# A retention block and a dense block in one kernel: loading order and order of work of the first microseconds

## The chip, the cores and the metric

The kernel runs on one core of a Trainium2 chip. The metric is the device time of one execution in microseconds; three runs of the kernel before gave 627.72, 628.25 and 628.29, median 628.25. The profile comes from one execution of its own, which took 627.76.

The engines in the views: PE is TensorE's matmul and PEld its weight load, DVE is VectorE, ACT ScalarE, POOL GpSimd, SP SyncE, which issues most of the DMAs. "Batch" below is one of the four batch entries.

## The reference

Four batch entries of 768 tokens with 8 heads of 64 pass a recurrent retention, then a dense block of 512 to 2048 to 512 with a leaky ReLU between. All is float32, but the weights arrive as float64 and are turned into float32 on the chip.

```python
gamma = 1.0 - 2.0 ** (-5.0 - np.arange(H, dtype=np.float32))
for t in range(S):
    state = gamma[None, :, None, None] * state + np.einsum('bhd,bhe->bhde', k[:, :, t], v[:, :, t])
    y[:, :, t] = scale * np.einsum('bhd,bhde->bhe', q[:, :, t], state)
x = np.ascontiguousarray(attn_out.transpose(0, 2, 1, 3)).reshape(B * S, H * D)
h = x @ w_in
g = np.maximum(0.01 * h, h)
out = g @ w_out
```

## The kernel before

The tokens are cut into six chunks of 128 for each batch. A chunk's output is a sum of two parts: tokens of earlier chunks through the state, and tokens of its own chunk through scores, q times k masked by causality, times v. The decay is taken out of the products: v is scaled by a table that depends on head and token (`decay_v`, L160), and the result by another (`gq`, in `tokens_taken`, L303). Both tables are made on the chip from a small input, `decay`, of 8 rows of 948 numbers, one row for each head. Matmuls with selector rows spread them over the 128 partitions: three small ones into `tables` (L934 to L938), copied by ScalarE into `dec` (L941), and one of 512 columns into `spread` (L946), copied into the front of `dec` (L950). These matmuls contract over all 128 partitions, so the 120 partitions without a head are set to zero.

The first chunk, on which the change works, has no state yet. For each batch b: `score(0,b)` is 32 small matmuls, `masked(0,b)` one VectorE operation of 128x768 out of PSUM, `decay_v(0,b)` scales v in place on GpSimd, `values(0,b)` are 32 matmuls of the masked scores with v, and `taken(0,b)` moves the result through VectorE, times gq, into the dense block's input x. Scores and values share two PSUM rooms (tag "att") in turn, so that a score of a later batch reuses the room of an earlier value once that is taken.

The weights come in pieces of 512 KB of float64. ScalarE makes the exponents of a piece (`next_powers`, three activations: L595, L599, L600). VectorE makes the mantissas: `begin_mantissas` is L607 and L612, with a given operation in between; `end_mantissas` is L619, which needs ScalarE's exponents, and then issues the load of a later piece. `next_mantissas` is both.

Most of the kernel uses Strassen-like schemes for the dense block, but the first quarter of the hidden units of chunk 0 is computed plainly by `direct` (L701), in four steps; step n reads weight piece n, and each call of `next(steps)` puts one step of four matmuls of 256 columns (two batches of 128) into PE's order. `th` says which two batches.

The schedule is written out by hand (`manual_schedule`): each engine executes its own instructions in the order of the program, and waits come from the data. The order at the start of the program is thus what the change edits. The loads of L882 to L901 go out on SP's queue in the order of the program, the decay rows on ScalarE's. `keep_busy` (L914) puts matmuls on zeros into PE's order while nothing has arrived.

Of the kernel before, what the change touches and what calls it, by code (L numbers as in the profile page):

```python
# [15 lines left out]
AF = mybir.ActivationFunctionType  # L16
# [6 lines left out]
def kernel(  # L23
# [14 lines left out]
    nc = tc.nc  # L38
    NC = S // C
    DM = H * D  # L40
    HP = H // 2
    NU = DF // 512
    N = B * C // 2
# [15 lines left out]
    dec = const.tile([128, HP * C + NC * H + HP], FP32, name="dec")  # L59
# [27 lines left out]
    def block(k, i):  # L87

        if k < N_UNITS - 1:
            return unit(k)[:, PLACE.get(i, i) if k % 2 else i]  # L90
        return units[k][i // 2][:, i % 2] if i < 6 else last_s4[:, 0]
# [3 lines left out]
    step = dec[:, HP * C + NC * H :]  # L95
# [24 lines left out]
    def load_qk(c, b, queue=nc.sync):  # L120
        queue.dma_start(out=heads[c, b][0], in_=qk[c, b])

    def load_v(c, b, queue=nc.sync):
        queue.dma_start(out=heads[c, b][1][:, 1], in_=kv[c, b][:, 1])
# [35 lines left out]
    def decay_v(c, b, engine=nc.gpsimd, behind=None):  # L160
        v = vals[c, b] if c >= JOINED else heads[c, b][1][:, 1]
        if engine is not nc.scalar:
            op = engine.tensor_tensor(out=v, in0=v,  # L163
                                      in1=gk[c].unsqueeze(2).to_broadcast([128, H, D]),
                                      op=ALU.mult)
            if behind is not None:
                tc.add_manual_dep(op.ins, behind.ins.name, IN_ORDER, reason="one port for both")
        else:
            for h in range(H):
                engine.activation(v[:, h], v[:, h], AF.Identity, scale=gk[c][:, h : h + 1])  # L170
# [9 lines left out]
    def score(c, b):  # L180

        ps = two_banks(f"ap_{c}_{b}").rearrange("p j a t -> p j (a t)")[:, :, 0:NS]
        scores[c, b] = ps.rearrange("p j (m n t) -> p j m n t", n=3, t=C // 2)
        scores_to(heads[c, b][0], [scores[c, b][:, j] for j in range(2)])
# [29 lines left out]
    def masked(c, b):  # L214
        am = new_am(c, b)
        nc.vector.tensor_tensor(
            out=am.rearrange("p j m n t -> p j m (n t)"),
            in0=scores[c, b].rearrange("p j m n t -> p j m (n t)"),
            in1=mask.rearrange("p n t -> p (n t)").unsqueeze(1).unsqueeze(1)
                .to_broadcast([128, 2, HP // 2, 3 * C // 2]), op=ALU.mult)  # L220
        scores[c, b] = am
# [20 lines left out]
    def values(c, b):  # L242
        if (c, b) not in sums_at:
            sums_at[c, b] = apart(two_banks(f"yp_{c}_{b}"))
        last_values(c, b)
        first_values(c, b)
# [51 lines left out]
    def taken(c, b, xb):  # L298

        tokens_taken(c, b, xb)  # L300
        state_taken(c, b, for_state(sums_at[c, b]))
# [232 lines left out]
    def load_piece(n, place=None):  # L534
        if n >= N_PIECES:
            return
        if not f64:
            nc.sync.dma_start(out=piece(n), in_=weights[n].rearrange("p (h n) -> p h n", h=2))
            return
        if place is None:  # L540
            tag, bufs = ("raw", 3) if n < N_PIECES - 4 else (("qk", "kv")[n % 2], AHEAD)
            raws[n] = work.tile([128, W], I64, tag=tag, bufs=bufs, name=f"raw{n}")
        else:
            raws[n] = place.bitcast(I64)
        nc.sync.dma_start(out=raws[n], in_=weights[n])

    def next_powers(scratch=None, between=None):
        n = done["powers"]
        done["powers"] += 1
        if n < N_PIECES and f64:  # L550
            powers(n, scratch, between)
        elif between is not None:
            between()

    def begin_mantissas(between=None):

        mantissas_begun(done["mantissas"], between)

    def end_mantissas():
        n = done["mantissas"]  # L560
        done["mantissas"] += 1
        op = mantissas_ended(n)
        if n != 3:
            load_piece(n + 4 if n < 3 else n + 3)
        if n == N_PIECES - 1:
            new_pair(2)
            for b in range(2):
                heads[2, b] = [work.tile([128, 2, HP, C], FP32, tag="qk", bufs=AHEAD,
                                         name=f"qk_2_{b}")]
            load_qk(2, 0)  # L570
            load_qk(2, 1)
            of_pair(2, 0, 1)
            of_pair(2, 0, 0)
        if n % 4 == 3 and n > 7:
            add_sums(n // 4)
        return op
# [121 lines left out]
    def temp(name, at):  # L698
        return work.tile([128, 2, N], FP32, tag=name, name=f"{name}_{at}")

    def direct(c, u, x, g, th):  # L701

        banks = [ffs.tile([128, 2, N], FP32, tag="ff", bufs=4, name=f"d{r}_{c}_{th}")
                 for r in range(2)]
        for step in range(4):
            kh, k = divmod(step, 2)
            for r in range(2):
                for i in range(2):
                    nc.tensor.matmul(  # L709
                        banks[r][:, i, :], lhsT=block(2 * u, r + 2 * kh)[:, k, ts(i, 128)],  # L710
                        rhs=x[:, 2 * kh + th, k, :], start=(step == 0 and i == 0),
                        stop=(step == 3), skip_group_check=True)
                if step == 3:
                    nc.scalar.activation(g[:, 2 * r + th], banks[r], AF.Prelu, alpha=0.01)
            yield

    filled = mask.rearrange("p n t -> p (n t)").bitcast(BF16)[:, 0:C]

# [159 lines left out]
    x, t = xs[0]  # L878
    rows = t[:, 1:3].rearrange("p i k n -> p (i k n)")[:, 0 : decay.shape[1]]
    nothing = t[:, 0, 0, 0:64].bitcast(BF16)  # L880
    half = decay.shape[1] // 2
    load_qk(0, 0)  # L882
    load_qk(0, 1)
    nc.vector.memset(t[:, 0, 0, 0:64], 0.0)
    nc.gpsimd.memset(rows[:, :half], 0.0)
    nc.vector.memset(rows[:, half:], 0.0)
    nc.scalar.dma_start(out=rows[0:H], in_=decay)
    load_v(0, 0)
    load_v(0, 1)
    load_piece(0)  # L890
    load_piece(1)
    load_qk(0, 2)
    load_v(0, 2)
# [10 lines left out]
    for s in range(2):  # L904
        part = mask[ts(s, 64), 0 : 3 - s : 2 - s]
# [4 lines left out]
    parts = [new_g(0, 0)]  # L910
# [3 lines left out]
    def keep_busy(n):  # L914
        for _ in range(n):
            nc.tensor.matmul(idle.rearrange("p i (two n) -> p (i two) n", two=2), lhsT=nothing,
                             rhs=nothing.unsqueeze(1).to_broadcast([128, 4, 128]),
                             start=True, stop=True, skip_group_check=True)
# [3 lines left out]
    n_gq = HP * C  # L922
# [5 lines left out]
    def scratch(name, n):  # L928
        return work.tile([128, 2, N], FP32, tag=name, name=f"{name}_x{n}")

    keep_busy(10)
    score(0, 0)
    n_gk, n_old = NC * H, JOINED * H
    nc.tensor.matmul(tables[:, 0, 0:n_old], lhsT=by_head, rhs=powers_of[:, 0:n_old], start=True,  # L934
                     stop=True, skip_group_check=True)
    nc.tensor.matmul(tables[:, 0, n_old:n_gk], lhsT=in_order, rhs=powers_of[:, n_old:],
                     start=False, stop=True, skip_group_check=True)
    nc.tensor.matmul(tables[:, 0, n_gk : n_gk + HP], lhsT=place, rhs=g_step, start=False,  # L938
                     stop=True, skip_group_check=True)
    masked(0, 0)  # L940
    nc.scalar.copy(out=dec[:, n_gq:], in_=tables[:, 0, 0 : n_gk + HP])  # L941
    decay_v(0, 0)
    score(0, 1)
    decay_v(0, 1)
    masked(0, 1)
    nc.tensor.matmul(spread.rearrange("p i n -> p (i n)"), lhsT=place, rhs=g_q, start=True,  # L946
                     stop=True, skip_group_check=True)
    values(0, 0)
    values(0, 1)
    nc.scalar.copy(out=dec[:, 0:n_gq], in_=spread.rearrange("p i n -> p (i n)"))  # L950
    next_powers(scratch("m5", 0))
    begin_mantissas(lambda: taken(0, 0, x))
    taken(0, 1, x)
    end_mantissas()
    next_powers(scratch("u2", 1))
    score(0, 2)
    steps = direct(0, 0, x, parts[0][1], 0)
    next(steps)
    converted = next_mantissas()
    decay_v(0, 2, behind=converted)  # L960
# [760 lines left out]
def _decay(H, D, NC):  # L1721

    import numpy as np

    lg = np.log1p(-(2.0 ** (-5.0 - np.arange(H))))
    t = np.arange(1, C + 1)
    gq = np.exp(lg[:, None] * t[None, :]) / math.sqrt(D)
    gq = gq.reshape(H // 4, 2, 2, C).transpose(1, 2, 0, 3).reshape(2, -1)
    step = np.exp(C * lg).reshape(H // 4, 2, 2).transpose(1, 2, 0).reshape(2, -1)
    place = np.concatenate([np.repeat(np.eye(2), 64, axis=1), gq, step], axis=1)  # L1730
    place = np.concatenate([place, np.zeros((H - 2, place.shape[1]))])
    in_order = np.exp(-lg[:, None] * t[None, :])
    by_head = in_order.copy()
    by_head[swapped(H)] = np.roll(by_head[swapped(H)], C // 2, axis=1)
    powers = [np.diag(np.exp(-c * C * lg)) for c in range(NC)]
    return np.concatenate([by_head, in_order, *powers, place], axis=1).astype(np.float32)

def _layout(q, k, v, w_in, w_out):

# [63 lines left out]
```

## Time and profile before

| | us |
|---|---|
| median of three runs | 628.25 |
| the profiled execution | 627.76 |
| its span, first to last instruction | 625.9 |
| matrix engine (PE) busy in the span | 620.0 |
| VectorE busy | 520.0 |
| ScalarE busy | 285.5 |
| GpSimd busy | 147.4 |

A span has 1.86 us less than the profiled execution's own time; the rest is before the first and after the last instruction. In a timeline a line gives the start from the beginning of the span, the length, the engine, the line of the program, the operation, what is written and read, and in brackets the time in which the engine stood idle before it and what ended that. In the list of waits a line gives the engine and the line that waited, what it waited for, the microseconds in total, the number of times and the longest. In the chain of waits a line gives start, length and what was under way in that stretch.

The transfers of the first microseconds, from the trace's DMA view (issue, and microseconds from issue to landing; for the two v blocks the trace was asked in pairs, so the smaller and the larger value stand):

| transfer | KB | issued | to landing |
|---|---|---|---|
| qk of batch 0 | 512 | 0.80 | 3.6 |
| qk of batch 1 | 512 | 1.25 | 4.8 |
| decay rows (ScalarE's queue) | 29.6 | 1.59 | 4.69 |
| v of batch 0 | 256 | 1.72 | 5.2 |
| v of batch 1 | 256 | 2.19 | 6.1 |
| weight piece 0 | 512 | 2.66 | 6.9 |
| weight piece 1 | 512 | 3.18 | 7.7 |
| qk of batch 2 | 512 | 3.67 | 8.5 |
| v of batch 2 | 256 | 4.41 | 8.4 |

### The profile page before, as it was taken

How to read it: one execution, taken by the hardware profiler on the slowest of the kernel's cores; microseconds unless marked ns; L12 is line 12 of the kernel's file. 1: busy time of each engine (PE TensorE's matmuls, PEld its weight loads, DVE VectorE, ACT ScalarE, POOL GpSimd, SP SyncE). 2: the span in 40 equal slices, each digit the busy share in tenths (PEclk: the TensorE clock that was granted, in tenths of full speed). 3: DMA queues.
4: the chain of work that ended last, by engine and by line, in shares of the span. 5: the costliest groups of instructions: out<-in, count | busy, mean ns of one | idle time of the engine just before them, and what ended most of it. 6: DMA issues, size and time to landing. Idle time of an engine off the chain costs nothing.

```text
span 625.9 us, 15366 instructions
## 1 busy us (share of the span) xinstructions
PE 620.0 (99%) x6410; PEld 571.8 (91%) x6410; DVE 520.0 (83%) x799; ACT 285.5 (46%) x546; POOL 147.4 (24%) x152
## 2 busy tenths in 40 slices
PE   8999999999999999999999999999999999999998
PEld 5888888888888889998999999999999999999997
DVE  5689769889979976779888868789968789989897
ACT  4876556347444114352433433634614435545641
POOL 2000000000010110105133052331250711379473
PEclk9999999999999999999999999999999999999999
DMA  8941426547772996496976996988478568688601
GB/s 324 403 154 42 127 68 215 159 144 231 259 282 75 327 362 248 130 349 198 334 232 205 292 335 235 327 277 283 148 262 268 174 226 266 207 276 290 206 3 67
DMA packets 105940, 141.00 MB, mean 225 GB/s; under 512 B 4488, under 2 KB 84232, under 8 KB 105872
## 3 DMA queue, kind: packets, MB, share of 16 engines
q1 hardware_dynamic: 105712, 139.94, 67.2%
q8 instruction: 50, 0.82, 0.5%
q14 instruction: 18, 0.15, 0.1%
q10 hardware_dynamic: 160, 0.10, 0.0%
HBM read 113.54 MB, written 26.48 MB: 224 GB/s over the span
## 4 chain that ended last, share of the span: by engine, by line
PE 98%; DMA 1%; DVE 0%; issue 0%; DVEq 0%
PE bank L1497 28%; PE bank L1342 14%; PE bank L688 10%; PE bank L1457 8%; PE C_h L688 4%; PE B_o L688 4%; PE A_h L688 4%; PE C_o L688 4%; PE A_o L688 4%; PE B_h L688 4%; PE d L709 2%; PE D_h L688 2%; PE D_o L688 2%; PE bank L374 1%; PE bank L456 1%; PE bank L385 1%
## 5 line engine op out<-in xcount | busy, mean ns | idle before, releaser
L623 DVE TENSOR_TENSOR made<-made,bank 128x512 f32<-128x512 f32 (+1 forms) x96 | 55.8, 617 | 33.0 <-PE bank L1497 29.3
L1497 PE MATMUL bank<-x,wb 128*128 128x128 f32 x672 | 78.5, 276 | 0.0
L1497 PEld LDWEIGHTS bank<-x,wb 128*128 128x128 f32 x672 | 77.3, 192 | 1.2 <-ACT bank L1501 0.2
L626 DVE TENSOR_TENSOR g<-g 128x512 f32<-128x512 f32 x96 | 66.0, 708 | 4.7 <-ACT g L1539 0.5
L1497 PE MATMUL bank<-x,wa 128*128 128x128 f32 x512 | 67.7, 275 | 0.0
L1497 PEld LDWEIGHTS bank<-x,wa 128*128 128x128 f32 x512 | 62.7, 192 | 0.3
L1501 ACT COPY bank<-bank 128x512 f32<-128x512 f32 (+1 forms) x32 | 16.6, 518 | 92.0 <-PE bank L1497 88.3
L623 DVE TENSOR_TENSOR g<-made 128x512 f32<-128x512 f32 x64 | 51.8, 830 | 3.3 <-DVE made L623 0.5
L1497 PE MATMUL bank<-t,wa 128*128 128x128 f32 x384 | 53.3, 275 | 0.0
L1342 PE MATMUL bank<-g,w 128*128 128x128 f32 x392 | 50.5, 276 | 0.0
L1497 PEld LDWEIGHTS bank<-t,wa 128*128 128x128 f32 x384 | 48.0, 192 | 0.0
L1342 PEld LDWEIGHTS bank<-g,w 128*128 128x128 f32 x392 | 46.8, 192 | 0.1
L1539 ACT ACTIVATE g<-g 128x512 f32<-128x512 f32 x64 | 38.1, 634 | 7.6 <-DVE g L623 7.6
L688 PE MATMUL bank<-g,w 128*128 128x256 f32 x168 | 38.0, 382 | 0.0
L1312 POOL TENSOR_TENSOR x<-g 128x512 f32<-128x512 f32 x12 | 17.0, 1419 | 88.9 <-DVE x L626 34.4
L1457 PE MATMUL bank<-g,w 128*128 128x256 f32 x168 | 37.8, 382 | 0.0
L163 POOL TENSOR_TENSOR in<-in,dec 128x512 f32<-128x512 f32 x3 | 3.7, 1232 | 144.2 <-DMA in<-in_kv_dram 139.2
L1457 PEld LDWEIGHTS bank<-g,w 128*128 128x128 f32 x168 | 31.4, 190 | 4.3
L688 PEld LDWEIGHTS bank<-g,w 128*128 128x128 f32 x168 | 31.3, 190 | 4.2
L623 DVE TENSOR_TENSOR o<-o,bank 128x512 f32<-128x512 f32 (+2 forms) x43 | 26.2, 632 | 10.2 <-ACT bank L806 4.3
L420 POOL MEMSET between<- 128x1 f32 x16 | 1.9, 117 | 130.8 <-PE bank L456 102.4
L623 DVE TENSOR_TENSOR o<-o,w 128x2048 f32<-128x2048 f32 (+2 forms) x16 | 27.4, 1731 | 0.2
(283 smaller groups left out, 1348.4 us busy)
## 6 DMA issues: line engine op xcount, KB each, us to landing
wa<-kept SPq DMA_DIRECT2D x16, 1344.0 KB, 8.5
w<-leaf_kept SPq DMA_DIRECT2D x44, 448.0 KB, 5.0
raw<-in_weights_dram SPq DMA_DIRECT2D x31, 512.0 KB, 4.3
wb<-kept SPq DMA_DIRECT2D x16, 896.0 KB, 6.3
wa<-kept SPq DMA_DIRECT2D x16, 448.0 KB, 4.6
wb<-kept SPq DMA_DIRECT2D x16, 448.0 KB, 6.9
out_dram<-o SPq DMA_DIRECT2D x23, 256.0 KB, 3.3
qk<-in_qk_dram SPq DMA_DIRECT2D x11, 512.0 KB, 8.2
```

The source lines that it names most:

```text
L374: nc.tensor.matmul(at[j][ts(h, 64), n, m, i], lhsT=x[ts(j, 64), 1, a, ts(h, 64)], rhs=x[ts(j, 64), 0, a, ts(h, 64)], start=(n == 0 and a = ...
L385: nc.tensor.matmul(sums[h][ts(j, 64), n, a], lhsT=key[ts(h, 64), 2 * a + j], rhs=val[ts(h, 64), 2 * a + j], start=(n == 0 and a == 0), sto ...
L623: return nc.vector.tensor_tensor(out=out, in0=a, in1=b, op=ALU.add)
L626: return nc.vector.tensor_tensor(out=out, in0=a, in1=b, op=ALU.subtract)
L688: nc.tensor.matmul(to, lhsT=block(w, sa)[:, k, ts(i, 128)], rhs=rhs[:, k, a:z], start=(first and (i == 0 or split) and n == 0 and k == 0), ...
L709: nc.tensor.matmul(banks[r][:, i, :], lhsT=block(2 * u, r + 2 * kh)[:, k, ts(i, 128)], rhs=x[:, 2 * kh + th, k, :], start=(step == 0 and i ...
L1312: op = nc.gpsimd.tensor_tensor(out=out, in0=a, in1=b, op=ALU.subtract)
L1342: nc.tensor.matmul(ps[q][:, to], lhsT=weights[i][j], rhs=moving[i][s], start=(i == 0 and m in ("M1", "M5", "M4")), stop=True, skip_group_c ...
L1457: nc.tensor.matmul(room[x][:, i, :], lhsT=block(2 * u + 1, sa)[:, k, ts(i, 128)], rhs=rhs[:, k, :], start=(first and i == 0 and k == 0), s ...
L1497: nc.tensor.matmul(ps[q][:, i], lhsT=w[:, j, i], rhs=part_of(moving[i], s), start=(i == 0 and m in ("M1", "M5", "M4")), stop=True, skip_gr ...
L1501: nc.scalar.copy(out=ps[3], in_=ps[0])
L1539: nc.scalar.activation(g[:, i], g[:, i], AF.Prelu, alpha=0.01)
```

## The change

The decay input gets 24 rows of zeros, so that it has 32. All 32 are loaded by one DMA, issued right after the first qk load; the zeros of the other partitions are then written in four memsets over partitions 32 to 63 and 64 to 127, which don't touch the rows that are loaded. In the loads, v of batch 0 and weight piece 0 come ahead of qk and v of batch 1.

The order of work changes too. Six matmuls on zeros stand at PE's head in place of ten. The tables are made ahead of the first score. Batch 0 passes through its mask, its values and its `taken` first, together with the conversion of weight piece 0; batch 1 follows behind. Step 0 of `direct` is cut into two halves of 128 columns, one for each batch: the first half stands ahead of the values of batch 1, the second behind the score of batch 2. The later steps are as before.

```diff
-    def direct(c, u, x, g, th):
+    def direct(c, u, x, g, th, by_batch=False):
...
         for step in range(4):
             kh, k = divmod(step, 2)
-            for r in range(2):
-                for i in range(2):
-                    nc.tensor.matmul(
-                        banks[r][:, i, :], lhsT=block(2 * u, r + 2 * kh)[:, k, ts(i, 128)],
-                        rhs=x[:, 2 * kh + th, k, :], start=(step == 0 and i == 0),
-                        stop=(step == 3), skip_group_check=True)
...
-            yield
+            n_parts = 2 if by_batch and step == 0 else 1
+            for part in range(n_parts):
+                at = ts(part, N // n_parts)
+                for r in range(2):
+                    for i in range(2):
+                        nc.tensor.matmul(
+                            banks[r][:, i, at], lhsT=block(2 * u, r + 2 * kh)[:, k, ts(i, 128)],
+                            rhs=x[:, 2 * kh + th, k, at],
+                            start=(step == 0 and part == 0 and i == 0),
+                            stop=(step == 3), skip_group_check=True)
...
+                yield
...
     load_qk(0, 0)
+    nc.scalar.dma_start(out=rows[0:32], in_=decay)
+    nc.vector.memset(t[:, 0, 0, 0:64], 0.0)
+    for a, z in ((32, 64), (64, 128)):
+        nc.gpsimd.memset(rows[a:z, :half], 0.0)
+        nc.vector.memset(rows[a:z, half:], 0.0)
+    load_v(0, 0)
+    load_piece(0)
     load_qk(0, 1)
-    nc.vector.memset(t[:, 0, 0, 0:64], 0.0)
-    nc.gpsimd.memset(rows[:, :half], 0.0)
-    nc.vector.memset(rows[:, half:], 0.0)
-    nc.scalar.dma_start(out=rows[0:H], in_=decay)
-    load_v(0, 0)
     load_v(0, 1)
-    load_piece(0)
     load_piece(1)
...
-    keep_busy(10)
-    score(0, 0)
     n_gk, n_old = NC * H, JOINED * H
+    keep_busy(6)
     nc.tensor.matmul(tables[:, 0, 0:n_old], lhsT=by_head, rhs=powers_of[:, 0:n_old], start=True,
                      stop=True, skip_group_check=True)
...
+    nc.scalar.copy(out=dec[:, n_gq:], in_=tables[:, 0, 0 : n_gk + HP])
+    score(0, 0)
     masked(0, 0)
-    nc.scalar.copy(out=dec[:, n_gq:], in_=tables[:, 0, 0 : n_gk + HP])
     decay_v(0, 0)
+    nc.tensor.matmul(spread.rearrange("p i n -> p (i n)"), lhsT=place, rhs=g_q, start=True,
+                     stop=True, skip_group_check=True)
+    nc.scalar.copy(out=dec[:, 0:n_gq], in_=spread.rearrange("p i n -> p (i n)"))
+    values(0, 0)
+    next_powers(scratch("m5", 0))
+    begin_mantissas(lambda: taken(0, 0, x))
+    end_mantissas()
     score(0, 1)
     decay_v(0, 1)
     masked(0, 1)
-    nc.tensor.matmul(spread.rearrange("p i n -> p (i n)"), lhsT=place, rhs=g_q, start=True,
-                     stop=True, skip_group_check=True)
-    values(0, 0)
+    steps = direct(0, 0, x, parts[0][1], 0, by_batch=True)
+    next(steps)
     values(0, 1)
-    nc.scalar.copy(out=dec[:, 0:n_gq], in_=spread.rearrange("p i n -> p (i n)"))
-    next_powers(scratch("m5", 0))
-    begin_mantissas(lambda: taken(0, 0, x))
     taken(0, 1, x)
-    end_mantissas()
     next_powers(scratch("u2", 1))
     score(0, 2)
-    steps = direct(0, 0, x, parts[0][1], 0)
     next(steps)
     converted = next_mantissas()
     decay_v(0, 2, behind=converted)
...
-    return np.concatenate([by_head, in_order, *powers, place], axis=1).astype(np.float32)
+    table = np.concatenate([by_head, in_order, *powers, place], axis=1)
+    return np.concatenate([table, np.zeros((32 - H, table.shape[1]))]).astype(np.float32)
```

More of the change, by code (lines that the diff above doesn't have):

```diff
@@ L706, in direct @@
             kh, k = divmod(step, 2)
-            for r in range(2):
-                for i in range(2):
-                    nc.tensor.matmul(
-                        banks[r][:, i, :], lhsT=block(2 * u, r + 2 * kh)[:, k, ts(i, 128)],
-                        rhs=x[:, 2 * kh + th, k, :], start=(step == 0 and i == 0),
-                        stop=(step == 3), skip_group_check=True)
-                if step == 3:
-                    nc.scalar.activation(g[:, 2 * r + th], banks[r], AF.Prelu, alpha=0.01)
-            yield
+            n_parts = 2 if by_batch and step == 0 else 1
[8 more added lines that the diff above has]
+                            stop=(step == 3), skip_group_check=True)
+                    if step == 3:
+                        nc.scalar.activation(g[:, 2 * r + th], banks[r], AF.Prelu, alpha=0.01)
+                yield
     filled = mask.rearrange("p n t -> p (n t)").bitcast(BF16)[:, 0:C]
```

## The prediction, made before the changed kernel was run

> **What bounds the kernel now.** I read the page's engine shares first, then the matrix engine's waits, then the chain of waits in order of time for the first 30 us, then VectorE's own timeline there. The shares and the full list of the matrix engine's waits over the whole span:
>
> ```profile
> PE 620.0 (99%) x6410; PEld 571.8 (91%) x6410; DVE 520.0 (83%) x799; ACT 285.5 (46%) x546; POOL 147.4 (24%) x152
> ...
> PE ap L196 <- DVE x L311: 1.1, 1, 1.1
> PE idle L916 <- DVE t L884: 1.1, 1, 1.1
> PE tables L934 <- DMA t<-decay_dram: 0.8, 1, 0.8
> ```
>
> TensorE is the bound and all three of its waits lie in the first 12.3 us. After that it is busy to the end, so what the change does to the time is the shift of the point from which PE runs on without waiting. The chain shows that point (start, length, what):
>
> ```profile
> 1.59 4.69 DMA t<-decay_dram
> ...
> 6.41 0.37 PE tables L934 x2
> ...
> 7.22 0.81 PE ap L196 x24
> 8.03 1.07 PE spread L946 x2
> 9.10 0.62 PE yp L266 x16
> 9.72 0.43 PE yp L255 x16
> ...
> 10.25 0.69 DVE x L311
> ...
> 12.26 0.89 PE ap L196 x22
> 13.14 3.67 PE d L709 x16
> ```
>
> L709 x16 is dense steps 0 and 1, 1.84 us each: step 0 at 13.14, step 1 at 14.97. The wait before 12.26 is put down to VectorE (taken(0,1), done 12.14), but score(0,2) also needs the third qk block, issued at 3.67 with 8.5 us to landing, 12.17. The two coincide; I hold the transfer for the true one, since the PSUM room score(0,2) reuses was freed by taken(0,0) at 10.94. Step 1 needs the second weight piece, which VectorE finishes late:
>
> ```profile
> 9.58 0.43 DVE L607 TENSOR_SCALAR w<-raw 128x512 uint32<-128x512 uint32 x1 [0.49 <-DMA raw<-in_weights_dram]
> 10.25 0.69 DVE L311 TENSOR_TENSOR x<-yp,dec 128x512 f32<-128x512 f32 x1 [0.24 <-PE yp L255]
> 10.86 0.68 DVE L612 SCALAR_TENSOR_TENSOR w<-raw,w 128x512 f32<-128x512 uint32 x1
> 11.45 0.69 DVE L311 TENSOR_TENSOR x<-yp,dec 128x512 f32<-128x512 f32 x1
> 12.05 0.68 DVE L619 SCALAR_TENSOR_TENSOR w<-w,z 128x512 f32<-128x512 f32 x1
> 12.65 0.42 DVE L607 TENSOR_SCALAR w<-raw 128x512 uint32<-128x512 uint32 x1
> 13.11 0.69 DVE L612 SCALAR_TENSOR_TENSOR w<-raw,w 128x512 f32<-128x512 uint32 x1
> 13.91 0.69 DVE L619 SCALAR_TENSOR_TENSOR w<-w,z 128x512 f32<-128x512 f32 x1
> ```
>
> VectorE runs from 9.58 (first weight piece lands) to 14.60 with 0.24 us of idle: five microseconds of work without a hole, 0.37 us ahead of the step that needs it. That row of eight operations is what I price the change against.
>
> [...] The stand-in matmuls on 512 columns follow each other by 0.42 us until 3.59 and by 0.23 from 3.97:
>
> ```profile
> 3.16 0.15 PEld L916 LDWEIGHTS <-t 128*128 128x128 bf16 x1 [0.28 <-issue]
> 3.59 0.15 PEld L916 LDWEIGHTS <-t 128*128 128x128 bf16 x1 [0.27 <-issue]
> 3.97 0.31 PEld L916 LDWEIGHTS <-t 128*128 128x128 bf16 x2 [0.23 <-issue]
> ```
>
> so the switch came near 3.95, after 2.9 us of work (from 1.05). The page's clock row says 1.00 throughout and doesn't show it. [...] here they were issued at 1.59 to 2.19, their 16 packets moved between 5.0 and 5.5, and they landed at 6.28, after the second qk block (1.25 + 4.8 = 6.05). The trace says order of issue, and I use that.
>
> **The change part by part.**
>
> *Decay rows.* They no longer wait for the memset that ends at 1.49, and are issued about 0.8, beside the first qk block (0.80). They are four times as large: 4 x 29.6 = 118 KB, at the 405 GB/s of this stretch 0.30 us. The first qk block lands at 0.80 + 3.6 = 4.4. In order of issue: 4.4 + 0.30 + 0.15 (6.28 less 6.05, less the old rows' 0.07) = 4.85; tables 0.13 later as now (6.28 to 6.41), at 5.0 instead of 6.41. Bounds: ahead of the qk block, about 3.7; behind the first v block (256 KB, 0.6 us, or 0.9 at the 230 to 320 GB/s of 5.5 to 7.5 us), 5.7. The zeros take two memsets more: POOL 0.49, VectorE 0.45 us. They hide, since the mask, which now follows them on both (done near 2.9 instead of 2.43), is first read after 6.8.
>
> *Loads.* Ahead of the first piece stand 680 KB less (2078 to 1398 KB with it): 1.7 us at 405 GB/s, up to 2.3 at 300, so it lands at 7.3 to 7.9 instead of 9.56. The second qk block comes behind it, about 9.2, its v block about 9.8. All that follows shifts by the extra 89 KB, 0.2 us: the third qk block 12.4. Eight transfers stand in flight: the ninth, v(0,2), is issued at 4.41 as the first lands at 4.4, and so on; the new order starves none. No queue receives another instruction than before except these.
>
> *The order of work.* Before, both batches' scores and values ran first and VectorE's masks (0.96 each) were done at 9.09, in time in which it had nothing else. Now mask(0,1) stands behind the conversion of piece 0, and the conversion waits for ScalarE. Followed through with the durations above:
> - tables 5.0, their 0.81 (6.41 to 7.22); score(0,0) 5.81, 0.83; spread 6.64, 1.07, to 7.71.
> - ScalarE copies gq, 0.59, to 8.34, and starts piece 0's powers 0.11 before that end as now; three activations, 9.62 to 11.64 = 2.02, give the exponents at 10.25. Piece 0 has landed by then.
> - mask(0,0) 6.86 to 7.82, values(0,0) 7.9 to 8.95, taken(0,0) 9.05, first product to 10.3: not the bound. score(0,1) 9.2 to 10.05, decay of v(0,1) on POOL to 10.9: hidden.
> - L619 of piece 0 at 10.3; mask(0,1) 0.6 later, 10.9 to 11.86. PE meanwhile does dense step 0 for batch 0, 11.0 to 11.9 (eight passes on 128 columns; later in the chain 56 such of L1497 take 6.25, 0.112 each).
> - values(0,1) 11.95, 1.05, to 13.0; taken(0,1) 13.1. Here VectorE idles 1.2 us. Behind it on its queue stand L607, L612, L619 of piece 1; from taken to the end of L619 is 2.55 as now (0.60 + 0.46 + 0.80 + 0.69): 15.65. Step 1 at 15.75.
> - score(0,2) 13.0 and the second half of step 0, 13.9 to 14.8, are done and PE waits 0.9.
>
> Step 1 at 15.75 against 14.97: **0.8 us later**. What is gained, piece 0 earlier by 1.7 to 2.3, is spent on a serial chain across four engines. The halves themselves cost 16 x 0.112 = 1.8 for 1.84, nothing. From step 1 on every consumer is late by the same: mask(0,2) 15.6, piece 2's end 18.6 for a step 2 at 19.3, v(0,3) scaled by 20.9 for values at 22.3. PE has no later wait that could give it back.
>
> *Six stand-in matmuls for ten.* They end at 1.05 + 6 x 0.425 = 3.6, before the 3.95 at which the clock rose, and PE then stands still until 5.0. The cover that hid a slow start before (PE's early work waited for transfers up to 12.2) is gone, since that work is now the head of the chain. If the clock has not risen, PE needs another 2.9 us of work, to 7.9, and of the 2.71 us of tables, score and spread it loses at most 1.45. At least 0: [...]. I take half, **0.7**, since only spread streams 512 columns and the tables move 4 to 32.
>
> Sum: +0.8 + 0.7 = +1.5. The profiled execution took 627.76 (span 625.9 and 1.86 around it), so 629.3 for one like it; the median of the runs shown, 628.25, is 0.5 above, so 629.7.
>
> **The rivals.**
> - *Warm clock.* The gap of 1.4 us is too short for the clock to matter, or the rise comes at 3.6. For: 2.55 us of work is near 2.9. Then +0.8: 629.05, 628.6 to 629.5.
> - *No slower: the decay rows overtake.* [...] tables run straight behind the stand-ins, the array stays warm, score(0,0) starts at 4.6 as now. The chain would be 1.2 earlier at its head, but then piece 0's landing (7.6) starts the powers in place of 8.23, so 0.6 of it counts: step 1 at 15.1, +0.1: 628.4, 626.9 to 628.6 if piece 0 lands sooner too. It decides from a landing of the rows below 4.2. Against: the packets at 5.0 to 5.5.
> - *Late rows.* Served behind the first v block, 5.7: +0.85 more with the clock cold: 630.6, to 631.4.
>
> **How the numbers follow.** Forecast 0.47, 629.7, 629.1 to 630.5; warm 0.30; overtaking 0.13; late 0.10. What a measurement can tell from no change is 0.2%, 1.26 us: above 629.5 slower, below 627.0 faster. Slower: 0.37 + 0.04 + 0.10 = 0.51. Same: 0.10 + 0.26 + 0.09 = 0.45. Faster: 0.04 from overtaking. The range takes in warm and most of late, and the near end of overtaking: 628.3 to 631.2.
>
> **What would show it.** Right: tables near 5.0; VectorE's mask of (0,1) behind L619, ending near 12 (13 cold); a hole of 1.2 us before taken(0,1); PE waiting before the second dense step, which starts at 15.7 or later; score(0,0)'s 32 matmuls longer than 0.90. Wrong: tables at 4 or sooner; the second dense step before 15; a total below 628.3, or a later hole in PE that takes the shift up.

## The result and the profile after

The changed kernel takes 630.83 us (median; the times go from 629.39 to 632.18), the kernel before 628.15 (627.72 to 628.73) in the same runs: ratio 1.0041, 95% interval 1.0027 to 1.0055. It is slower by 2.7 us, and its times spread over 2.8 us where those of the kernel before spread over 1.0. The profiled execution took 631.88, its span is 630.0; of the eight shown it is the second slowest, so its trace shows a bad case and not the median.

The page's engine shares of the changed kernel:

```profile
PE 622.5 (99%) x6414; PEld 573.8 (91%) x6414; DVE 520.3 (83%) x800; ACT 285.4 (45%) x546; POOL 148.3 (24%) x153
```

TensorE is the bound as before. The span is 4.1 us longer; 1.6 of that is time outside its busy time (7.5 us for 5.9), and 2.5 is longer busy time, although it has four matmuls on zeros fewer. The list of its waits over the whole span (waited for, us in total, times, longest) says where:

```profile
PE d L712 <- DVE w L619: 2.2, 2, 1.5
PE idle L921 <- DVE t L888: 1.1, 1, 1.1
PE tables L938 <- DMA t<-decay_dram: 1.0, 1, 1.0
```

The wait of 1.1 us before the score of batch 2 is gone. In its place PE waits 2.2 us, before the first half of dense step 0 and before step 1, for L619, the end of a piece's conversion. The chain of waits shows what came in between (start, length, what):

```profile
0.80 3.90 DMA t<-decay_dram
...
4.83 0.58 PE tables L938 x2
...
6.25 1.48 PE ap L196 x24
7.72 2.02 PE spread L948 x2
9.74 1.05 PE yp L266 x16
10.79 0.68 PE yp L255 x16
...
11.57 0.69 DVE x L311
12.26 0.61 DVE w L612
...
12.96 0.70 DVE w L619
...
13.71 1.16 PE d L712 x8
14.87 0.61 PE yp L266 x16
15.48 0.43 PE yp L255 x16
...
15.94 0.69 DVE x L311
...
18.55 1.99 PE d L712 x8
```

Two things are to be seen. Tables begin 1.6 us sooner than before (4.83 for 6.41), but from then on the chain runs through PE, VectorE, PE, VectorE, PE, one after another, to dense step 1 at 18.55, 3.6 us later than the 14.97 of before. And the same matmuls are longer: spread 2.02 us for 1.07, the values of batch 0 1.05 and 0.68 for 0.62 and 0.43. The values of batch 1, at 14.87, are back at 0.61 and 0.43. VectorE's timeline shows the other side (the bracket is the idle time before an operation):

```profile
8.76 0.42 DVE L607 TENSOR_SCALAR w<-raw 128x512 uint32<-128x512 uint32 x1
11.57 0.69 DVE L311 TENSOR_TENSOR x<-yp,dec 128x512 f32<-128x512 f32 x1 [2.40 <-PE yp L255]
12.18 0.68 DVE L612 SCALAR_TENSOR_TENSOR w<-raw,w 128x512 f32<-128x512 uint32 x1
12.96 0.69 DVE L619 SCALAR_TENSOR_TENSOR w<-w,z 128x512 f32<-128x512 f32 x1
13.57 0.95 DVE L216 TENSOR_TENSOR am<-ap,mask 128x768 f32<-128x768 f32 x1
15.94 0.69 DVE L311 TENSOR_TENSOR x<-yp,dec 128x512 f32<-128x512 f32 x1 [1.42 <-PE yp L255]
```

Where the row had 0.24 us of idle before, it now has 2.40 ahead of taken(0,0) and 1.42 ahead of taken(0,1). The mask of batch 1 (L216 at 13.57) stands behind L619. What L619 waits for is the row of VectorE's own operations before it, taken(0,0) and L612, and through them the values of batch 0. ScalarE's exponents, which it needs too, were done at 12.25, 0.7 us before it began:

```profile
11.62 0.63 ACT L600 ACTIVATE z<-z 128x512 uint16<-128x512 int16 x1
```

The matrix engine's order is 3.7 us late at the values of batch 2 and stays so: 3.6 at 298 us, 4.0 at the last stage at 611 us.

### The profile page after: what moved, and what is told of

Same layout as the page of the kernel before. It is cut to its first block, busy times and chain, and to the rows that moved or that the text cites. A ratio compares the mean times of both kernels' runs of the same rounds, so it can differ in the third digit from the quotient of the medians.

```text
span 630.0 us, 15378 instructions
## 1 busy us (share of the span) xinstructions
PE 622.5 (99%) x6414; PEld 573.8 (91%) x6414; DVE 520.3 (83%) x800; ACT 285.4 (45%) x546; POOL 148.3 (24%) x153
## 4 chain that ended last, share of the span: by engine, by line
PE 98%; DVE 1%; DMA 1%; issue 0%; DVEq 0%
PE bank L1503 28%; PE bank L1348 14%; PE bank L688 10%; PE bank L1463 8%; PE C_h L688 4%; PE B_o L688 4%; PE A_h L688 4%; PE C_o L688 4%; PE A_o L688 4%; PE B_h L688 4%; PE d L712 2%; PE D_h L688 2%; PE D_o L688 2%; PE bank L456 1%; PE bank L374 1%; PE bank L385 1%
```

## The experiments

All are timed against the kernel before. "Stand-ins" are the matmuls on zeros of `keep_busy`. An array at full clock is called warm and one at the low clock cold; what tells them apart is spread, 1.07 us warm and 2.02 cold in the chain of waits, 1.12 and 2.07 in a timeline. The granted clock is 0.51 beside a spread of 2.07 in the trace of six stand-ins in the kernel before; in the changed kernel it stays at 1.00 beside the same length, so that cold is there read from the lengths. An edit is shown in part, against the kernel that its paragraph names.

**Ten stand-ins in the changed kernel.**

```diff
-    keep_busy(6)
+    keep_busy(10)
```

> The changed kernel with ten stand-in matmuls in place of six. Theory (serial chain plus a clock that is still low): the ten end at about 4.8, as the decay rows land, so the array works without a pause and the clock rises near 4; tables, score and spread then take 0.8, 0.83 and 1.07 us instead of 1.35, 1.5 and 2.0, dense step 1 starts at 15.7 instead of 18.5, and the time is that of the kernel before plus 0.8: about 629.0, with a spread between runs of about 1 us instead of 2.8. Rival (the clock is not what costs; the loads or the chain alone make the loss): 630.5 to 631 with the same spread.

Measured: 631.01 (629.94 to 632.25), ratio 1.0048 (1.0035 to 1.006). As a statement on the median the theory failed: ten don't help. But its trace, 630.34, is warm from score(0,0) on, and step 1 is late all the same:

```profile
1.05 4.45 PE L921 MATMUL idle<-t 128*128 128x512 bf16 x10 [1.05 <-DVE t L888]
5.29 0.45 PE L938 MATMUL tables<-t 128*128 128x16 f32 x2
...
7.24 1.13 PE L948 MATMUL spread<-t 128*128 128x512 f32 x2
...
16.75 1.99 PE L712 MATMUL d<-x,w 128*128 128x256 f32 x8 [0.70 <-DVE w L619]
```

The stand-ins now end as late as 5.5, because the clock rose later in this execution (the ten took 4.45 us for the 3.73 of the kernel before, and score(0,0) at 6.41 is the first at the warm length, 0.90), and tables stand behind them. Step 1 is at 16.75, 1.8 us later than before and 1.0 later than forecast: tables begin 0.3 late and, still cold in part, take 1.1 us for the 0.7 of a warm trace below, and the chain behind the values of batch 0 is 0.3 longer than forecast. The median is explained in part only. Two of the five executions, 631.01 and 631.13, have a mean granted clock of 0.997, which a fall like that in the next two versions would give; the slowest, 632.25, has 1.000 and no trace. A fixed number of stand-ins thus doesn't decide whether the array is warm.

**Six stand-ins in the kernel before.**

```diff
-    keep_busy(10)
+    keep_busy(6)
```

> The kernel before with six stand-in matmuls in place of ten, nothing else changed. Theory: its early work on the matrix engine waits for transfers up to 12.2 us, so a low clock there is mostly covered: 628.2, at most 0.5 more. Rival (a low clock costs what it costs, wherever it is): 2 us more, 630, as in the changed kernel.

Measured: 630.13 (629.18 to 631.55), ratio 1.0036 (1.0024 to 1.0049). The rival is right: four stand-ins fewer cost the kernel before 2.3 us, as much as the whole change. Its trace shows a part of how, in a table by stretches of 3.5 us (length, PE's busy time and instructions, granted clock, DMA share, GB/s):

```profile
4.00:7.50 3.50, 2.00 (x54) 1.00 1.02 338
7.50:11.00 3.50, 3.50 (x42) 0.51 1.00 399
11.00:14.50 3.50, 2.60 (x91) 1.00 1.03 406
```

The array had been warm at 4.34 (score(0,0) took 0.90, as before). Then it was busy for only 2.0 of 3.5 us, and from 7.5 to 10.9 us it had half its clock, although it was busy all through. Spread fell into that stretch: 2.07 us in its timeline. So the clock also falls again, for a stretch of 3.4 us, after a stretch with pauses. What sets the fall off isn't shown. The cover I had claimed for the kernel before wasn't there: VectorE's row of eight waited 0.24 us for values(0,0) already, so PE's early work was on the path and not covered up to 12.2. In this trace taken(0,0) comes at 11.80 instead of 10.25. But the trace is of the fastest of the five executions, 629.18, so it accounts for 1.3 of the 2.3 us; the three slowest have a mean clock of 0.999 to 1.000 and no trace, and whether they were cold from the start, as the changed kernel was, is open.

**The loads alone.** The padded rows and the new loading order in the kernel before, its order of work kept; the edit is against the kernel before.

```diff
     load_qk(0, 0)
+    nc.scalar.dma_start(out=rows[0:32], in_=decay)
...
+    load_v(0, 0)
+    load_piece(0)
     load_qk(0, 1)
...
```

> The padded decay rows and the new loading order alone, with the order of work and the ten stand-ins of the kernel before. Theory: score(0,1) now stands in the matrix engine's order ahead of spread and waits for the second qk block, which lands at 8.6 instead of 6.05; spread, the copy of gq and the exponents of piece 0 are 1.5 us later, and dense step 1 starts at about 15.9: 629.0. Rival (an earlier weight piece 0 is a gain by itself): about 627.4.

Measured: 629.73 (628.82 to 631.57), ratio 1.003 (1.0022 to 1.0039). An earlier weight piece is no gain by itself. The trace is of the slowest of its thirteen executions, 631.57. The list of PE's waits names the cause that was expected:

```profile
PE ap L196 <- DMA qk<-in_qk_dram: 1.5, 1, 1.5
```

and in the table by stretches the one after the pause has half the clock again:

```profile
5.00:8.40 3.40, 1.95 (x42) 1.00 1.04 407
8.40:11.80 3.40, 3.40 (x34) 0.51 1.02 400
```

The other executions fit a fall that costs more than a microsecond. Each execution has a mean granted clock over its whole span; half the clock for 3.4 us lowers it by 0.003. In nine executions it is 1.000, and they take 628.82 to 629.95, median 629.23, 1.4 us more than the kernel before and near the 629.0 expected. In four, the traced one among them, it is 0.994 to 0.997, and they take 630.62 to 631.57.

**The order of work alone.** The changed kernel with the loads and the rows of the kernel before, and ten stand-ins; the head of the edit against the kernel before, the rest of the order is that of the changed kernel.

```diff
-    keep_busy(10)
-    score(0, 0)
...
+    keep_busy(10)
     nc.tensor.matmul(tables[:, 0, 0:n_old], lhsT=by_head, rhs=powers_of[:, 0:n_old], start=True,
...
+    score(0, 0)
     masked(0, 0)
...
```

> The new order of work alone, with ten stand-ins, and the decay rows and loads of the kernel before. Theory (the loads are what lets the new order begin early; the order itself is the loss): tables wait for the rows until 6.4, the chain runs from there, dense step 1 starts near 17.5 warm: 630.5 to 631 in warm runs, 632 to 633 in cold ones, which are more frequent, since the array stands idle for a microsecond before tables. Rival (the loads are the loss, the new order is neutral): 628 to 629.

Measured: 631.89 (630.5 to 634.03), ratio 1.0066 (1.0052 to 1.008). Its trace, 630.5, is warm and has dense step 1 at 17.59, as worked out. The order is a loss by itself, and so are the loads. That the loads give part of the order's loss back is seen in the traces, 17.59 for the 16.75 with the new loads and ten stand-ins; in the times (medians 631.89 and 631.01) the ranges overlap.

**The changed kernel again, twice, for its trace.** No edit.

> The changed kernel once more, for a second trace. Theory: where the clock rises differs between executions, so the time lies anywhere from 629.4 to 632.2 and goes with the length of tables, score and spread in its trace: each microsecond that these take longer is a microsecond in the time. Rival (another cause of the spread, such as transfers): tables, score and spread take 1.4, 1.5 and 2.0 us again whatever the time.

> The changed kernel a third time, for its trace. Theory: if tables, score and spread run warm (0.8, 0.83, 1.07 us) the time is near 629.5; if cold (1.35, 1.5, 2.0), 631 to 632. Rival: the time doesn't go with these lengths.

Measured: 631.16 and 631.34, both cold, spread 2.07 in both timelines. With the first profile that makes three cold traces, at 631.16 to 631.88. No trace of the changed kernel fell at its low end of 629.4, so that a warm array makes that end isn't shown on the kernel itself. Its variants point to it: 629.32 to 630.34 in the warm traces of the versions below and above with its loads and ten stand-ins.

**No stand-in at all in the changed kernel.**

```diff
-    keep_busy(6)
```

> The changed kernel without any stand-in. Theory ([...] the changed kernel's runs lie between a warm end near 629.4 and a cold end near 632): with none the array is always cold from tables through spread, so the runs gather at the cold end, 631.5 to 633, and none is below 631. Rival (the stand-ins don't set the clock in the head, the spread has another cause): the same median and spread as with six, 630.8 and 629.4 to 632.2.

Measured: 631.29 (630.67 to 631.37), ratio 1.005 (1.0038 to 1.0063). The spread shrank from 2.8 to 0.7 us and the low times are gone, as the theory has it; the cold end lies lower than I had put it, with the median 0.2 below the 631.5 and one run, 630.67, below the 631 (tables start 0.24 sooner here, at 4.59). Spread takes 2.07 in its trace. Always cold is thus hardly worse than the median with six: if the theory is right, six stand-ins buy a warm array only in some executions.

**Ten stand-ins, and four in the gap before dense step 0.**

```diff
-    keep_busy(6)
+    keep_busy(10)
...
+    keep_busy(4)
     steps = direct(0, 0, x, parts[0][1], 0, by_batch=True)
```

> The changed kernel with ten stand-ins at the head and four more in the matrix engine's gap between score(0,1) and the first half of dense step 0. Theory (part of the loss is the clock falling again [...], part is the serial chain): with the gap filled the clock stays up more often, so the median comes down from 631.0 to about 630.3, the time of the trace with ten stand-ins in which every matmul ran warm, and the spread shrinks. Rival (after ten stand-ins the clock costs no more; all that is left is the chain): 631.0 with the same spread.

Measured: 630.18, ratio 1.0046 (1.003 to 1.0062). The times fall into two groups, 629.46, 629.69, 629.99 and 630.36 against 632.42 and 632.72. The median is the one expected, but the spread did not shrink. The warm trace, 629.69, has tables at 4.88, close to the 5.0 of the forecast, and can be laid beside it step by step:

```profile
9.20 1.04 POOL L163 TENSOR_TENSOR kv<-kv,dec 128x512 f32<-128x512 f32 x1 [2.10 <-DMA kv<-in_kv_dram]
...
9.51 1.28 DVE L612 SCALAR_TENSOR_TENSOR w<-raw,w 128x512 f32<-128x512 uint32 x1
...
10.90 0.69 DVE L619 SCALAR_TENSOR_TENSOR w<-w,z 128x512 f32<-128x512 f32 x1
...
11.64 1.16 PE L712 MATMUL d<-x,w 128*128 128x128 f32 x8 [1.17 <-DVE w L619]
```

L612 took 1.28 us instead of 0.68: GpSimd scaled v(0,1) from 9.20 to 10.24, and L612 ended 0.55 after that. Wherever the two meet and GpSimd begins first, here and in the versions below with the mask ahead and with step 0 whole, L612 takes 1.28, 1.41 and 0.78 us and each time ends 0.53 to 0.56 us behind GpSimd. How GpSimd holds it up isn't shown. In the kernel before both scalings were over at 9.64, before L612. In the cold traces of the changed kernel itself they don't meet either: L612 begins at 12.18 in the first, GpSimd ends at 10.36.

**GpSimd's scaling held back.** As the version with the gap filled, but the scaling of v(0,1) waits for the end of piece 0's conversion.

```diff
-    end_mantissas()
+    first = end_mantissas()
     score(0, 1)
-    decay_v(0, 1)
+    decay_v(0, 1, behind=first)
```

> The changed kernel with ten stand-ins, four more in the gap, and GpSimd's scaling of v(0,1) held back until piece 0's conversion has ended. Theory (GpSimd's scaling from 9.2 to 10.24 held up VectorE's first product, which took 1.28 us instead of 0.68 in the trace with the gap filled): the product takes 0.68 again, dense step 1 starts 0.6 earlier, at about 15.9, and warm runs are near 629.1 instead of 629.6. Rival (the product waited for something else): 1.28 again and the same time, 629.5 to 630.

Measured: 632.14 (629.88 to 632.37), ratio 1.0065 (1.0052 to 1.0079). The trace, 629.88 and warm, shows the local effect:

```profile
9.61 0.68 DVE L612 SCALAR_TENSOR_TENSOR w<-raw,w 128x512 f32<-128x512 uint32 x1
10.40 0.69 DVE L619 SCALAR_TENSOR_TENSOR w<-w,z 128x512 f32<-128x512 f32 x1
```

and step 1 at 16.01 for 16.48. The time doesn't confirm it: the four other times are 631.8 and more, without a trace, and the warm one loses 0.9 us again by the last stage, 0.3 of it to a wait for GpSimd at 463 us. That the scaling held up L612 is shown (0.68 us apart from it for 1.28 beside it); that holding GpSimd back saves time isn't.

**The mask ahead of the conversion's end.** As the version with the gap filled, with VectorE's and PE's order changed.

```diff
-    begin_mantissas(lambda: taken(0, 0, x))
-    end_mantissas()
+    begin_mantissas()
+    taken(0, 0, x)
     score(0, 1)
     decay_v(0, 1)
     masked(0, 1)
+    end_mantissas()
...
+    values(0, 1)
     steps = direct(0, 0, x, parts[0][1], 0, by_batch=True)
     next(steps)
-    values(0, 1)
-    taken(0, 1, x)
+    begin_mantissas(lambda: taken(0, 1, x))
...
-    converted = next_mantissas()
+    converted = end_mantissas()
```

> As the kernel with the gap filled, but mask(0,1) stands ahead of the end of piece 0's conversion on VectorE, values(0,1) ahead of the first half of dense step 0, and piece 1's first product ahead of taken(0,1). Theory (serial chain): mask(0,1) no longer waits for ScalarE's exponents, dense step 1 starts near 15.5 instead of 16.75, and the time is 1.2 us less than with the gap filled alone: about 629.1. Rival (the chain isn't bound by the mask's place, but by loads or the clock): no difference to the kernel with the gap filled alone.

Measured: 629.47 (628.22 to 631.07), ratio 1.0021 (1.0013 to 1.0029), against 630.18 (from 629.46) with the gap filled alone. The lowest times differ by the 1.2 expected, the medians by 0.7. Its trace is a cold one: spread takes 2.07 us and values(0,0) start at 10.00, 2.3 later than in the warm trace above. Yet it has the second half of dense step 0 at 15.87, step 1 near 16.9, and 629.71 in all, the time of the warm trace above:

```profile
11.84 0.96 DVE L216 TENSOR_TENSOR am<-ap,mask 128x768 f32<-128x768 f32 x1
12.71 0.68 DVE L619 SCALAR_TENSOR_TENSOR w<-w,z 128x512 f32<-128x512 f32 x1
13.31 0.42 DVE L607 TENSOR_SCALAR w<-raw 128x512 uint32<-128x512 uint32 x1
14.08 0.69 DVE L311 TENSOR_TENSOR x<-yp,dec 128x512 f32<-128x512 f32 x1 [0.36 <-PE yp L255]
```

The hole before taken(0,1) is 0.36 us instead of 1.42, since mask, L619 and L607 now stand without a pause. So the three moves together, the mask ahead of L619, the values of batch 1 ahead of the first half and L612 ahead of taken(0,0), are worth about a microsecond, as the forecast said; what the mask's place alone is worth wasn't measured.

**Dense step 0 whole again.** The edit is against the version with the gap filled.

```diff
-    steps = direct(0, 0, x, parts[0][1], 0, by_batch=True)
-    next(steps)
     values(0, 1)
...
     score(0, 2)
+    steps = direct(0, 0, x, parts[0][1], 0)
     next(steps)
```

> As the kernel with the gap filled, but dense step 0 is whole again and stands behind score(0,2). Theory: the second dense step waits for VectorE's end of piece 1 either way, so the split neither gains nor costs: within 0.3 us of the kernel with the gap filled. Rival (the first half in front of values(0,1) is a gain of 0.9 us of matrix time): 0.9 us slower.

Measured: 629.66 (629.32 to 631.97), ratio 1.0033 (1.0022 to 1.0045), lowest 0.14 below the version with halves. The split gains nothing. The reason is not quite the one expected, as the matrix engine's timeline shows:

```profile
12.59 0.69 PE L266 MATMUL yp<-am,kv 128*64 128x64 f32 x16 [1.69 <-DVE am L216]
...
14.48 3.85 PE L712 MATMUL d<-x,w 128*128 128x256 f32 x16
```

The matrix engine now waits once, before the values of batch 1, for their mask. Step 1 follows step 0 without a pause, 0.1 us behind the end of piece 1's conversion; it starts at 16.4, and at 16.5 with the halves.

**A version meant to beat both.** The old order of work with both masks first, padded rows, piece 0 ahead of v(0,1), ScalarE's first activation ahead of the copy of gq, L612 ahead of taken(0,0), step 0 by batch ahead of score(0,2), and three stand-ins in front of it. The edit is against the changed kernel.

```diff
...
+    begin_mantissas()
+    next_powers(scratch("m5", 0), lambda: nc.scalar.copy(
+        out=dec[:, 0:n_gq], in_=spread.rearrange("p i n -> p (i n)")))
+    taken(0, 0, x)
     values(0, 1)
+    end_mantissas()
+    taken(0, 1, x)
...
```

> A version meant to beat both: the order of work of the kernel before, in which both masks come first, with the padded rows, piece 0 ahead of v(0,1), ScalarE's first activation on piece 0 ahead of the copy of gq, piece 0's first product ahead of taken(0,0), dense step 0 by batch ahead of score(0,2), and three stand-ins in the gap. Theory: VectorE's row of eight operations starts at 9.1 instead of 9.58 and dense step 1 at about 14.5 instead of 14.97: 627.4 to 627.8. Rival (the larger rows delay the qk blocks by as much as is gained, and the clock falls): 628.5 or more.

Measured: 628.84 (628.05 to 629.81), ratio 1.0013 (1.0006 to 1.0019). The rival is right in its number and its first part; a falling clock isn't seen, spread takes 1.12 us in this trace. score(0,0) starts at 5.35 instead of 4.71, since the first qk block lands 4.5 us after its issue instead of 3.6, and the matrix engine's list of waits has a new one, for v(0,1), which now comes behind piece 0:

```profile
PE yp L266 <- POOL kv L163: 1.0, 1, 1.0
```

Half of that microsecond is GpSimd and VectorE meeting again, the other way round, for L612 began at 9.25, just before GpSimd, which then took 1.55 us instead of 1.04:

```profile
9.29 1.55 POOL L163 TENSOR_TENSOR kv<-kv,dec 128x512 f32<-128x512 f32 x1 [0.83 <-DMA kv<-in_kv_dram]
```

No version tried beat the kernel before.

## Why the prediction was right

*What bounds, and that nothing gives a shift back.* Right. The shift at the values of batch 2 was 3.73 us in the profiled execution and 4.0 at the last stage.

*The decay rows.* The time was right (tables at 4.83 for 5.0) by luck, the reason was not. I held the order of issue for the rule; in fact the rows' packets moved from 2.5 us on, among those of the first qk block: 14 of their 48 lie between 2.5 and 3.0. Why the rows of the kernel before, issued 0.8 us later, moved only from 5.0 us on, behind the first qk block, is open. The price is on the other side: that block landed at 5.3 instead of 4.4. Here it is hidden, as score(0,0) stands behind tables; in the loads alone and in the version meant to beat both it wasn't. The rival that ended on the other side saw the overtaking but not that price, and put the rows' landing at 3.7 where it was 4.70.

*Piece 0 and the qk block of batch 1.* Piece 0 landed 5.6 us after its issue at 1.72, at 7.3, in the range given; the qk block at 8.6 for 9.2.

*The serial chain.* Right in kind, wrong in one link, and too small in size. The link is L619: I had put ScalarE's exponents (10.25) and VectorE's own row (10.3) nearly level and called the values of batch 0 and taken(0,0) not the bound. In every trace of the new order in which L619 stands right behind L612 the exponents are ready 0.26 to 0.88 us before it starts, and the chain runs from tables over score, mask (in the cold traces spread), values and taken(0,0) to L612 and L619. The size: +0.8 was forecast, the warm trace with tables at 4.88 has step 1 at 16.48 instead of 14.97, +1.5. Its L619 is 0.6 later than forecast, which is the 0.6 that L612 took longer beside GpSimd's scaling; I had called that scaling hidden because PE didn't wait for it, and not asked what it holds up on VectorE. Another 0.2 is the half of a dense step, 1.09 from start to start for the 0.9 I took from groups of 56. Where GpSimd and L612 don't meet, only the small part is left: from the end of the values of batch 0 to step 1 it is 7.1 us in the three traces of the changed kernel and in three warm ones, for the 6.80 forecast, and 7.7 in the warm trace where they meet.

*The six stand-ins.* Right in kind, and the mis-sized term. I gave 0.7, at most 1.45, by letting the clock rise after 2.9 us of work from tables on, near 7.9. In the profiled execution it was low until about 11.4 (score(0,1), from 11.21, took 1.00 us for 0.85 to 0.90 warm): from the start of tables to the end of the values of batch 0 it took 6.64 us for 3.95 forecast, +2.7. In the kernel before the clock rose near 3.95 and in the trace with ten stand-ins between 6.0 and 6.4; what sets the moment isn't shown, so that my 2.9 us of work was an estimate from a single trace. What it costs is a matter of each execution: if the low times are the warm ones, from nearly nothing (629.4) to 2.5 us (632). With no stand-ins, always cold, 631.29.

*The sum.* +1.5 was forecast, +2.7 measured at the median: about 1.5 for the chain, by the warm trace's 629.69, and the rest for the clock. That split is an estimate and rests on a variant, since no trace of the changed kernel itself was warm; in the profiled execution the clock is the larger part, 2.7 of the 3.6 us by which step 1 is late. The forecast "slower" and the range held, and the two terms it names are the ones found, both too small. That the range held is in part luck: 630.83 lies above the 629.1 to 630.5 of the forecast itself, where the rival of late rows stood, and the rows weren't late (4.70). Three of the eight executions are above 631.2.

*What stays open.* Later shifts of up to 1.1 us between 220 and 530 us, which differ between executions (0.7 in the trace with ten stand-ins, 1.1 in that of the loads alone), weren't traced to a cause beyond the wait for GpSimd named above. Why two of six executions with ten stand-ins and a filled gap still take 632.4 and more isn't known, since neither has a trace. The padded rows were not tried alone.

## What to carry to other kernels

Where the head of a kernel waits for transfers, an earlier transfer is worth only what the chain behind it can use: here 1.7 to 2.3 us of an earlier weight piece went into one batch passing back and forth between the matrix engine and VectorE, where two batches had filled each other's waits. In an engine's fixed order, put what needs a far-off result (a conversion's end) behind what is ready (the next mask); with two more moves that was worth about a microsecond here. And count stand-in matmuls as part of the design: fewer of them, or a pause after them, can cost as much as the edit under study, and the cost shows in a wider spread of times (2.4 us for 1.1 in the kernel before) as well as in the median.

## What the runs showed of the hardware that was not expected

- The matrix engine's clock falls again within microseconds: warm at 4.3 us, busy 2.0 of 3.5 us, then half clock for 3.4 us of full work (7.5 to 10.9). A clock row of 1.00 doesn't exclude a cold array at the start: in the changed kernel it says 1.00 while spread takes 2.02 us for 1.07.
- 32 rows of 3.7 KB, one to a partition, delayed a block of 512 KB issued at the same moment by 0.9 us: it took 4.5 us to land in the first trace of the changed kernel and in that of the version meant to beat both, which have different orders of the loads behind it, and 3.6 in the kernel before. That is three times the 0.3 that their 118 KB take at 405 GB/s. From 2 to 5 us the core moved 0.80 MB instead of 0.99 in the first trace.
- GpSimd's scaling of v(0,1), 1.04 us, lengthened VectorE's L612 from 0.68 to 1.28 us; where L612 began first, GpSimd's scaling took 1.55 for 1.04.
